# Summing the two halves of the attention output on GpSimd instead of VectorE, in a fused attention and expert kernel

## The chip, the cores and the metric

The kernel runs on one core of one Trainium2 chip. A core has engines with instruction queues of their own: TensorE (PE in the rows, with its weight loads as PEld), VectorE (DVE), ScalarE (ACT), GpSimd (POOL) and SyncE (SP), which here issues nearly all DMAs. Each queue runs strictly in order; engines wait for each other through semaphores. The metric is device time in microseconds (us); lower is better.

## The reference

Attention over 2 batches x 8 heads, 768 positions, head size 64. A position's bucket is the 6-bit sign pattern of its query (or key) times `proj`; a query sees only keys of its own bucket. Two expert layers follow.

```
mask   = q_bucket[:, :, :, None] == k_bucket[:, :, None, :]
scores = scale * q @ k.T, masked with -1e9, softmax over keys
x      = attn @ v                      # to 1536 tokens x 512
h      = (x @ w1) * (x @ w2) @ w3 @ w_out
out    = sum over e of p[:, e] * (relu(h @ e1[e]) @ e2[e])
```

## The kernel before

Every factor is split into a high and a low fp32r part (`hi`, `lo`), and products are made from two or three matmuls of those parts. The attention runs as 48 units (16 heads x 3 blocks of 256 queries). For unit `u`:

- `S` (PE): two tiles of 128 queries x 768 keys of scores into the two `s_ps` buffers. The mask bits sit in extra rows of the operands (`kb`, `ll`), so that a mismatch adds a huge number.
- `mx` (DVE, L443): copies the scores to `e` and takes the row minimum (signs are turned). `ex` (ACT, L446): exponential and row sum. `r1` (POOL, L459), `r2` (DVE, L461) and `en` (POOL L456, or ACT L455 for one tile in four): the normalisation.
- `T` (PE, L477): transposes of `e` into a `t_ps` buffer; `hi` (ACT, L483) and `lo` (DVE, L485) split them into `et`.
- `pv` (PE): twelve matmuls into the one `pv_ps` buffer. The weights are `vv`, which holds the high part of v in 64 columns and the low part in the next 64, so that rows 0 to 63 of `pv_ps` hold one half of the result and rows 64 to 127 the other.
- `po` (ACT, L502) copies the lower half to `pvs`; `xa` (DVE, L504) adds it to the upper half, straight from `pv_ps`, into the token matrix `xt`. The next unit's `pv` waits for `xa`.

Beside that, per head: SP loads q and k (`ld`) and v (`lv`, into `rv`), POOL scales and splits them (L368, L159, L162), and SP copies pieces between partitions (`k1`, `k2`, `k3`, `dq`, L344). Per two heads, `bm` makes the hash products, DVE turns them into bits (`is_pos`, L394), and SP spreads the bits (`mq`, `mk`). For the first head alone, DVE writes them in place. Eight pieces of expert weights are also loaded (`wraw`, L194) and split during the attention (ACT L196 and L208, DVE L198 to L211, POOL L162 and L214). Products of the first expert layer for the first 512 tokens (`fm`, 96 matmuls, tiles `xh` and `slot` into `t_ps` or `s_ps`) are the filler of PE near the end of the attention; `fc` and `fg` (L611) drain them. Then the attention's memory is freed and the expert layers run, first `xh` and `xl` (high and low part of `xt`, L153 and L156), then matmuls into `u_ps` and `o_ps`.

No order is written by hand. Every step is announced with an engine, a planned duration, what it depends on and a due time, which the table `RANK` shifts per group of steps. A list scheduler in `emit_all` then plays this through and emits the instructions in the order that comes out:

```
def op(key, eng, dur, fn, deps, prio, group=None):
    ...
    ops.append((eng, dur, fn, deps, prio + P * RANK.get(group, 0.0), group))
```

Of the kernel before, what the change touches and what calls it, by code (L numbers as in the profile page):

```python
# [13 lines left out]
AF = mybir.ActivationFunctionType  # L14
ALU = mybir.AluOpType
# [12 lines left out]
    "S0": -59.56,  # L28
    "S1": 3.69,
    "T0": -207.42,  # L30
    "T1": -82.6,
    "T2": -31.6,
    "b0": -57.56,
    "b1": -59.96,
    "bits": -7.65,
    "en": 2.75,
    "ex0": -95.56,
    "ex1": -444.49,
    "fd": -89.32,
    "fx": 240.7,  # L40
    "hi0": -7.87,
    "hi1": -248.41,
    "hi2": -157.19,
    "ld": -54.46,
    "lo0": -345.82,
    "lo1": -186.61,
    "lo2": -153.95,
    "lv": -53.81,
    "mx0": -264.79,
    "mx1": -0.59,  # L50
    "p0": -157.78,
    "p1": -422.6,
    "po": -405.44,
    "prep": 73.11,
    "pv": -5.01,
    "r1": -199.11,
    "r2": -270.42,
    "v": 180.48,
# [840 lines left out]
```

## Time and profile before

| | us |
|---|---|
| runs before: median (lowest, highest) of 3 | 1017.81 (1017.12, 1022.36) |
| the profiled execution: its own time | 1020.02 |
| the profiled execution: span from first to last instruction | 1018.2 |
| busy PE, DVE, ACT, POOL | 999.7, 510.1, 362.5, 307.8 |

The busy time is that of whole executions: PE works to the end, while the other engines have most of their work in the attention, which ends near 262 us. Matmuls are pipelined and their ends are modelled, so that a busy PE is not a PE at its peak. In rows on windows, each number of busy us is followed on the chip's page by a number of instructions in brackets; PEclk is the granted TensorE clock as a share of 2.4 GHz.

### The profile page before, as it was taken

What the parts mean: (1) busy time and instruction counts of PE and PEld (TensorE: products, weight loads), DVE (VectorE), ACT (ScalarE), POOL (GpSimd) and SP (SyncE); (2) the same over time, 40 slices, a digit from 0 to 9 for tenths busy, and PEclk for the clock granted to TensorE, in tenths of its full rate; (3) what the DMA queues carried; (4) which work ended last, traced back from release to release, by engine and by line L of the source; (5) the groups of instructions that cost most, each with busy time, mean ns of one, the idle gap of its engine ahead of it and who ended that gap; (6) DMA issues with size and microseconds to landing.
All of it is one profiled execution on the core that took longest, in us unless ns stands there. A gap on an engine that the chain in (4) does not pass through costs nothing.

```text
span 1018.2 us, 13166 instructions
## 1 busy us (share of the span) xinstructions
PE 999.7 (98%) x5035; PEld 844.6 (83%) x5035; DVE 510.1 (50%) x948; ACT 362.5 (36%) x669; POOL 307.8 (30%) x351
## 2 busy tenths in 40 slices
PE   7899999999999999999999999999999999999998
PEld 6888888988788888888888888888888888888886
DVE  6889999998599965954312212121121212212122
ACT  5889999988433322432201101101101101101100
POOL 6777788664000000074300064000650005300000
PEclk9999999999999999999999999999999999999999
DMA  6843544320034321332200032000220002001011
GB/s 162 184 128 77 130 121 112 82 80 21 1 116 127 119 94 49 117 103 63 63 1 1 1 93 73 0 1 1 78 88 1 1 1 73 31 1 42 1 42 42
DMA packets 51135, 64.12 MB, mean 63 GB/s; under 512 B 17688, under 2 KB 34072, under 8 KB 51072
## 3 DMA queue, kind: packets, MB, share of 16 engines
q1 hardware_dynamic: 50928, 63.27, 22.0%
q8 instruction: 40, 0.66, 0.3%
q14 instruction: 23, 0.19, 0.1%
q10 hardware_dynamic: 144, 0.01, 0.0%
HBM read 47.22 MB, written 3.15 MB: 49 GB/s over the span
## 4 chain that ended last, share of the span: by engine, by line
PE 82%; DVE 14%; DMA 1%; ACT 1%; issue 1%; POOL 1%; SPq 0%; DVEq 0%; ACTq 0%; POOLq 0%
PE u_ps L147 43%; PE o_ps L147 30%; DVE et L485 5%; DVE e L443 5%; PE s_ps L147 3%; PE pv_ps L147 2%; PE t_ps L477 2%; PE t_ps L147 2%; DVE xa L504 1%; DVE cbuf L211 1%; DMA wraw<-in_w 1%; ACT e L446 1%; DMA kb<-hh 0%; DVE cbuf L203 0%; DVE cbuf L206 0%
## 5 line engine op out<-in xcount | busy, mean ns | idle before, releaser
L819 DVE SCALAR_TENSOR_TENSOR hl<-u_ps,hl 128x512 fp32r<-128x512 f32 x96 | 66.4, 691 | 420.4 <-ACT hl L817 420.4
L817 ACT ACTIVATE hl<-u_ps 128x512 fp32r<-128x512 f32 x96 | 57.4, 598 | 459.3 <-PE u_ps L147 401.9
L147 PE MATMUL u_ps<-xh,slotl 128*128 128x512 f32 x936 | 220.6, 389 | 0.0
L147 PEld LDWEIGHTS u_ps<-xh,slotl 128*128 128x128 f32 x936 | 175.7, 188 | 36.5
L147 PE MATMUL u_ps<-xh,slot 128*128 128x512 f32 x696 | 165.0, 389 | 1.2 <-DVE xh L156 1.2
L147 PE MATMUL o_ps<-slotl,hl 128*128 128x512 f32 x648 | 154.7, 389 | 0.0
L147 PEld LDWEIGHTS u_ps<-xh,slot 128*128 128x128 f32 x696 | 130.6, 188 | 28.7 <-DVE xh L156 1.6
L147 PEld LDWEIGHTS o_ps<-slotl,hl 128*128 128x128 f32 x648 | 121.6, 188 | 25.2
L147 PE MATMUL o_ps<-slot,hl 128*128 128x512 f32 x504 | 119.9, 389 | 0.0
L147 PEld LDWEIGHTS o_ps<-slot,hl 128*128 128x128 f32 x504 | 94.6, 188 | 19.6
L159 POOL TENSOR_SCALAR slot<-wraw 128x512 fp32r<-128x512 f32 x28 | 17.8, 634 | 286.7 <-PE u_ps L147 269.7
L485 DVE TENSOR_TENSOR et<-t_ps,et 128x512 fp32r<-128x512 f32 x144 | 96.6, 680 | 5.8 <-ACT et L483 5.2
L446 ACT ACTIVATE e<-e,sm 128x768 f32<-128x768 f32 x96 | 89.5, 933 | 12.3 <-DVE e L443 11.0
L147 PE MATMUL pv_ps<-et,vv 128*128 128x256 f32 x576 | 92.8, 297 | 0.8 <-DVE xa L504 0.5
L443 DVE TENSOR_SCALAR_CACHE_REDUCE e<-s_ps 128x768 f32<-128x768 f32 x96 | 90.4, 945 | 4.9 <-PE t_ps L477 3.0
L477 PE MATMUL t_ps<-ident,e 128*128 128x128 f32 x576 | 87.0, 279 | 5.7 <-DVE et L485 4.0
L483 ACT ACTIVATE et<-t_ps 128x512 fp32r<-128x512 f32 x144 | 83.0, 592 | 12.5 <-PE t_ps L477 5.7
L159 POOL TENSOR_SCALAR slotl<-wraw 128x512 fp32r<-128x512 f32 x36 | 22.5, 624 | 208.8 <-PE u_ps L147 172.3
L477 PEld LDWEIGHTS t_ps<-ident,e 128*128 128x128 f32 x576 | 66.3, 142 | 15.9 <-DVE et L485 8.5
L147 PEld LDWEIGHTS pv_ps<-et,vv 128*128 128x128 f32 x576 | 76.0, 192 | 3.0 <-DVE xa L504 2.4
L456 POOL TENSOR_SCALAR e<-e,sm 128x768 f32<-128x768 f32 x72 | 65.5, 916 | 17.4 <-DVE sm L461 15.4
L147 PE MATMUL s_ps<-ka,hh 128*128 128x512 f32 x192 | 53.5, 360 | 3.8 <-issue 2.2
(111 smaller groups left out, 1092.9 us busy)
## 6 DMA issues: line engine op xcount, KB each, us to landing
wraw<-in_e SPq DMA_DIRECT2D x64, 256.0 KB
wraw<-in_w SPq DMA_DIRECT2D x16, 512.0 KB
wraw<-in_w3T SPq DMA_DIRECT2D x16, 512.0 KB
r<-in_qk SPq DMA_DIRECT2D x15, 384.0 KB
wraw<-in_w_out SPq DMA_DIRECT2D x8, 512.0 KB
rv<-in_v SPq DMA_DIRECT2D x16, 192.0 KB
out<-xa SPq DMA_DIRECT2D x12, 256.0 KB
ka<-hh SPq DMA_DIRECT2D x15, 192.0 KB
```

Of the source, the lines that this page charges most:

```text
L147: nc.tensor.matmul(out=o, lhsT=l, rhs=r, start=start, stop=stop)
L159: nc.gpsimd.tensor_scalar(out=o, in0=i, scalar1=1.0, scalar2=1.0, op0=ALU.mult, op1=ALU.mult)
L211: lambda: nc.vector.scalar_tensor_tensor(out=f(t), in0=lw.bitcast(U32), scalar=2.0 ** -52, in1=f(t), op0=ALU.mult, op1=ALU.mult)),
L443: op(("mx", u, t), "DVE", 873, lambda ps=ps, m=m, e=e: nc.vector.tensor_scalar(out=e, in0=ps[:, 0:S], scalar1=THR, scalar2=None, op0=ALU.m ...
L446: op(("ex", u, t), "ACT", 921, lambda e=e, m=m, rs=rs: nc.scalar.activation(out=e, in_=e, func=AF.Exp, scale=-1.0, bias=m, accum_out=rs), ...
L456: return "POOL", 872, lambda: nc.gpsimd.tensor_scalar(out=e, in0=e, scalar1=r[:, t:t + 1], scalar2=1.0, op0=ALU.mult, op1=ALU.mult)
L477: nc.tensor.transpose(out=ps[:, k, t * 128:(t + 1) * 128], in_=e_t[2 * (u % ER) + t][:, kt * 128:(kt + 1) * 128], identity=ident)
L483: op(("hi", n), "ACT", 480, lambda ps=ps, et=et: nc.scalar.activation(out=et[:, 0], in_=ps, func=AF.Copy), [("T", u, j), ("pv", n - NET)], Tj)
L485: op(("lo", n), "DVE", 602, lambda ps=ps, et=et: nc.vector.tensor_tensor(out=et[:, 1], in0=ps, in1=f(et[:, 0]), op=ALU.subtract), [("hi", ...
L504: op(("xa", u), "DVE", 340, lambda: nc.vector.tensor_tensor(out=xt[a, h // 2, t0:t0 + 256], in0=pv_ps[0:D], in1=pvs, op=ALU.add), [("po", ...
L817: op(("gh", n), "ACT", 480, lambda n=n, nu_=nu_: nc.scalar.activation(out=hl_t[n % 2][:, 0], in_=u_ps[nu_ % 4], func=AF.Relu), [ku] + hfre ...
L819: op(("uf", nu_), "DVE", 602, lambda n=n, nu_=nu_: nc.vector.scalar_tensor_tensor(out=hl_t[n % 2][:, 1], in0=u_ps[nu_ % 4], scalar=0.0, in ...
```

## The change

Four things change.

1. `po` now copies all 128 rows of `pv_ps` to a wider `pvs` (three buffers instead of two). A new step `pm` on SP moves the half that lies in the wrong partitions by a DMA from `pvs` to a new buffer `pvd` (two buffers). `xa` adds `pvs` and `pvd` on POOL instead of DVE. The next unit's `pv` waits for `po` alone.
2. v is rearranged on the host, so that `lv` reads 128 rows of 1.5 KB for a head instead of 768 rows of 256 bytes.
3. For the first head, the query bits are written in two pieces (256 columns, then 512), and the second head's low part `l` waits for the first piece. The scores of units 1 and 2 wait for the second.
4. All entries of `RANK` but two, many planned durations and the planned delay after a DMA (2300 ns before, 1900 now) differ, which gives all queues another order.

```diff
-    "xa": -317.88,
+    "pm": -125.95,
+    "xa": -29.47,
...
-    pvs_t = tiles(2, [64, 256], "pvs")
+    pvs_t = tiles(3, [128, 256], "pvs")
+    pvd_t = tiles(2, [128, 256], "pvd")
...
-            ("SP", 1460, [("cd", n - NRAW), ("c2", n - NRAW)], "cl",
+            ("SP", 2700, [("cd", n - NRAW), ("c2", n - NRAW)], "cl",
...
-        "SP": {"PE": 2300, "ACT": 2300, "DVE": 2300, "POOL": 2300, "SP": 2300, "NONE": 0},
+        "SP": {"PE": 1900, "ACT": 1900, "DVE": 1900, "POOL": 1900, "SP": 1900, "NONE": 0},
...
-                op(("l", hh), "DVE", 870, lambda: scaled_lo(nc.vector), [("h", hh)], T, g)
+                op(("l", hh), "DVE", 1000, lambda: scaled_lo(nc.vector), [("h", hh), ("mq", 0)], T, g)
...
-        op(("lv", hh), "SP", 600, lambda: nc.sync.dma_start(out=rv, in_=v[b, h].rearrange("(k p) d -> p k d", p=128)),
+        op(("lv", hh), "SP", 1000, lambda: nc.sync.dma_start(out=rv, in_=v[b, h].rearrange("p (k d) -> p k d", k=NK)),
...
-        op(("mq", 0), "DVE", 865, lambda: is_pos(lo[64:64 + PC], ps, q), [("mk", 0)], T, "b0")
-        keys[("sf", n)] = keys[("mq", 0)]
+        for i, (key, c) in enumerate(((("mq", 0), slice(0, 256)), (("sf", n), slice(256, S)))):
+            op(key, "DVE", (330, 600)[i], lambda c=c: is_pos(lo[64:64 + PC, c], ps, q, c), [("mk", 0)], T + i, "b0")
...
-            op(("pv", n), "PE", 472, lambda j=j: pv(j), [("lo", n), ("vl", hh), ("xa", u - 1), ("pv", n - 1)], Tp)
+            op(("pv", n), "PE", 472, lambda j=j: pv(j), [("lo", n), ("vl", hh), ("po", u - 1), ("pv", n - 1)], Tp)
...
-        op(("po", u), "ACT", 264, lambda: nc.scalar.activation(out=pvs, in_=pv_ps[D:2 * D], func=AF.Copy),
-           [("pv", NJ * u + NJ - 1), ("xa", u - 2)], Tp)
-        op(("xa", u), "DVE", 340, lambda: nc.vector.tensor_tensor(
-            out=xt[a, h // 2, t0:t0 + 256], in0=pv_ps[0:D], in1=pvs, op=ALU.add), [("po", u)], Tp)
+        w, t0 = h % 2, b * S + qp * 256
+        a, o = slice(w * D, (w + 1) * D), slice((1 - w) * D, (2 - w) * D)
+        op(("po", u), "ACT", 283, lambda: nc.scalar.activation(out=pvs, in_=pv_ps, func=AF.Copy),
+           [("pv", NJ * u + NJ - 1), ("xa", u - 3)], Tp)
+        op(("pm", u), "SP", 500, lambda: nc.sync.dma_start(out=pvd[a], in_=pvs[o]), [("po", u), ("xa", u - 2)], Tp)
+        op(("xa", u), "POOL", 520, lambda: nc.gpsimd.tensor_tensor(
+            out=xt[a, h // 2, t0:t0 + 256], in0=pvs[a], in1=pvd[a], op=ALU.add), [("pm", u)], Tp)
...
-        "v": v,
+        "v": v.reshape(v.shape[0], v.shape[1], -1, 128, D).swapaxes(2, 3).reshape(v.shape[0], v.shape[1], 128, -1),
```

What the new order looks like is shown at three places. The first is DVE's queue at the start: `ll_85` and `ll_86` are the low parts of heads 0 and 1, `kb_93` takes the key bits of head 0, and `e_99` the first scores. Before:

```order
L347 SCALAR_TENSOR_TENSOR ll_85<-r_114,svec,hh_81 128x768
L347 SCALAR_TENSOR_TENSOR ll_86<-r_115,svec,hh_82 128x768
L394 TENSOR_SCALAR kb_93<-s_ps_129,thr,amp 12x768
L394 TENSOR_SCALAR ll_85<-s_ps_129,thr,amp 12x768
L443 TENSOR_SCALAR e_99,sm_122<-s_ps_130 128x768
```

And in the changed kernel:

```order
L349 SCALAR_TENSOR_TENSOR ll_85<-r_117,svec,hh_81 128x768
L396 TENSOR_SCALAR kb_93<-s_ps_132,thr,amp 12x768
L396 TENSOR_SCALAR ll_85<-s_ps_132,thr,amp 12x256
L396 TENSOR_SCALAR ll_85<-s_ps_132,thr,amp 12x512
L349 SCALAR_TENSOR_TENSOR ll_86<-r_118,svec,hh_82 128x768
L446 TENSOR_SCALAR e_99,sm_125<-s_ps_133 128x768
```

The low part of head 1 has moved from ahead of the bits to behind them, and the query bits have become two instructions.

The second place is POOL's queue in the middle of the attention, around units 20 and 21, while the q and k of head 10 and the v of head 7 are split. `sm` is `r1`, `e` is `en`, `ll` and `hh` are the parts of q and k, `vv` those of v. Before:

```order
L459 TENSOR_SCALAR sm_124<-sm_124 128x2
L162 TENSOR_TENSOR ll_87<-r_114,hh_83 128x768
L456 TENSOR_SCALAR e_103<-e_103,sm_124 128x768
L159 TENSOR_SCALAR vv_98<-rv_116 128x6x64
L162 TENSOR_TENSOR vv_98<-rv_116,vv_98 128x6x64
L459 TENSOR_SCALAR sm_125<-sm_125 128x2
L456 TENSOR_SCALAR e_99<-e_99,sm_125 128x768
L456 TENSOR_SCALAR e_100<-e_100,sm_125 128x768
```

In the changed kernel:

```order
L510 TENSOR_TENSOR xa<-pvs_110,pvd_112 64x256
L164 TENSOR_TENSOR vv_98<-rv_119,vv_98 128x6x64
L462 TENSOR_SCALAR sm_127<-sm_127 128x2
L161 TENSOR_SCALAR hh_83<-r_117 128x768
L459 TENSOR_SCALAR e_103<-e_103,sm_127 128x768
L510 TENSOR_TENSOR xa<-pvs_111,pvd_113 64x256
L164 TENSOR_TENSOR ll_87<-r_117,hh_83 128x768
L462 TENSOR_SCALAR sm_128<-sm_128 128x2
L370 TENSOR_SCALAR r_118<-r_118,svec 128x768
L164 TENSOR_TENSOR xh_66<-xa,xh_66 128x512
```

One `xa` for each unit now stands among the same steps, and the `r1` and `en` of later units stand behind it.

The third place is PE's queue where the attention ends: the last `pv` (`vv_98`), the rest of the filler (`xh_66`), and the first product of the expert layers (`u_ps`). Before:

```order
L147 MATMUL pv_ps<-et_108,vv_98 128x256 x4
L147 MATMUL t_ps_134<-xh_66,slot_64 128x512 x12
L147 MATMUL s_ps_129<-xh_66,slot_64 128x512 x5
L147 MATMUL t_ps_134<-xh_66,slot_65 128x512 x12
L147 MATMUL s_ps_129<-xh_66,slot_64 128x512 x4
L147 MATMUL t_ps_134<-xh_66,slot_65 128x512 x12
L147 MATMUL u_ps_3041<-xh_3022,slot_62 128x512 x12
```

In the changed kernel:

```order
L149 MATMUL pv_ps<-et_108,vv_98 128x256 x4
L149 MATMUL t_ps_137<-xh_66,slot_63 128x512 x12
L149 MATMUL s_ps_132<-xh_66,slot_64 128x512 x5
L149 MATMUL t_ps_137<-xh_66,slot_64 128x512 x12
L149 MATMUL s_ps_132<-xh_66,slot_64 128x512 x5
L149 MATMUL t_ps_137<-xh_66,slot_65 128x512 x24
L149 MATMUL u_ps_3093<-xh_3074,slot_62 128x512 x12
```

58 filler matmuls instead of 45 are left behind the last `pv`, and the last two groups of twelve, which use one buffer, now follow each other directly.

## Rows read from the trace of the kernel before

**Rows 1.** The page: busy us (share of the span) xinstructions, by engine.

```profile
PE 999.7 (98%) x5035; PEld 844.6 (83%) x5035; DVE 510.1 (50%) x948; ACT 362.5 (36%) x669; POOL 307.8 (30%) x351
```

**Rows 2.** Windows: us, busy PE, PEld, DVE, ACT, POOL, PEclk, DMA, GB/s.

```profile
94.00:136.00 42.00, 40.64 (x294) 36.53 (x293) 41.71 (x89) 37.58 (x76) 34.32 (x41) 1.00 0.49 115
136.00:178.00 42.00, 41.18 (x305) 37.99 (x304) 41.61 (x91) 40.41 (x81) 34.30 (x42) 1.00 0.48 119
178.00:220.00 42.00, 41.65 (x299) 37.98 (x298) 41.66 (x90) 39.20 (x79) 27.52 (x34) 1.00 0.33 80
220.00:262.40 42.40, 41.90 (x288) 36.67 (x287) 36.22 (x72) 32.61 (x63) 18.18 (x24) 1.00 0.10 31
```

**Rows 3.** The chain that ended last, 100 to 112 us: start us, us, what.

```profile
104.01 1.20 DVE et L485 x2
105.21 0.33 DVE xa L504
...
108.83 0.42 DVE xa L504
```

**Rows 4.** Groups by line and shape, 94 to 220 us.

```profile
L485 DVE TENSOR_TENSOR et<-t_ps,et 128x512 fp32r<-128x512 f32 x77 | 51.7, 678 | 0.2
...
L504 DVE TENSOR_TENSOR xa<-pv_ps,pvs 64x256 f32<-64x256 f32 x26 | 10.7, 412 | 0.4
...
L162 POOL TENSOR_TENSOR ll<-r,hh 128x768 fp32r<-128x768 f32 x7 | 12.9, 1843 | 0.6
...
L162 POOL TENSOR_TENSOR xh<-xa,xh 128x512 fp32r<-128x512 f32 x2 | 2.6, 1298 | 0.0
...
L502 ACT ACTIVATE pvs<-pv_ps 64x256 f32<-64x256 f32 x26 | 9.9, 381 | 0.8
```

**Rows 5.** Timeline of the start: start us, us, engine, line, op.

```profile
5.92 1.02 DVE L347 SCALAR_TENSOR_TENSOR ll<-r,svec,hh 128x768 fp32r<-128x768 f32 x1 [1.33 <-ACT hh L352]
...
6.31 0.94 ACT L364 ACTIVATE hh<-r,svec 128x768 fp32r<-128x768 f32 x1 [0.42 <-DMA r<-in_qk]
...
7.28 2.17 DVE L347 SCALAR_TENSOR_TENSOR ll<-r,svec,hh 128x768 fp32r<-128x768 f32 x1 [0.34 <-ACT hh L364]
...
7.57 0.28 PE L147 MATMUL s_ps<-ll,pbh 128*128 128x256 f32 x1
...
8.66 0.94 ACT L358 ACTIVATE hh<-r,svec 64x768 fp32r<-64x768 f32 x1 [1.42 <-POOL ka L162]
...
11.71 0.62 PE L147 MATMUL s_ps<-kb,ll 76*128 76x512 f32 x2 [1.43 <-DVE ll L394]
...
12.37 0.96 DVE L443 TENSOR_SCALAR_CACHE_REDUCE e<-s_ps 128x768 f32<-128x768 f32 x1 [0.71 <-PE s_ps L147]
```

**Rows 6.** Timeline, 34 to 41 us.

```profile
34.80 0.52 SPq L344 DMA_DIRECT2D hh<-hh  x1
...
38.43 0.58 PE L147 MATMUL s_ps<-ka,hh 128*128 128x512 f32 x2 [2.16 <-issue]
```

**Rows 7.** Windows of the two stalls; columns as in rows 2.

```profile
36.00:42.00 6.00, 3.79 (x20) 3.29 (x19) 3.19 (x7) 2.24 (x5) 2.90 (x3) 0.81 1.11 217
66.00:69.00 3.00, 1.51 (x11) 1.01 (x9) 0.80 (x4) 1.13 (x2) 2.92 (x3) 1.00 0.29 63
```

**Rows 8.** Timeline, 60 to 76 us.

```profile
61.60 0.37 SPq L194 DMA_DIRECT2D wraw<-in_w  x1
...
67.87 0.67 ACT L196 ACTIVATE cbuf<-wraw 128x512 f32<-128x512 f32 x1 [2.66 <-DMA wraw<-in_w]
```

**Rows 9.** Timeline of the end of attention.

```profile
266.38 2.88 PE L147 MATMUL t_ps<-xh,slot 128*128 128x512 f32 x12
...
269.10 1.07 PE L147 MATMUL s_ps<-xh,slot 128*128 128x512 f32 x4
...
273.23 0.69 DVE L611 TENSOR_TENSOR g<-g,t_ps 128x512 f32<-128x512 f32 x1 [3.18 <-PE t_ps L147]
...
274.57 5.72 PE L147 MATMUL u_ps<-xh,slot 128*128 128x512 f32 x24 [1.22 <-DVE xh L156]
```

More of the change, by code (lines that the diff above doesn't have):

```diff
@@ L27 @@
     "CP": 16.1,
[L28 to L58, printed above, removed]
-    "xa": -317.88,
+    "S0": -71.69,
+    "S1": 65.66,
+    "T0": -210.57,
+    "T1": -24.46,
+    "T2": -166.93,
+    "b0": -120.38,
+    "b1": -78.37,
+    "bits": -313.13,
+    "en": -33.99,
+    "ex0": 115.81,
+    "ex1": -102.2,
+    "fd": -80.92,
+    "fx": 220.7,
+    "hi0": -232.84,
+    "hi1": -141.31,
+    "hi2": -183.33,
+    "ld": -79.23,
+    "lo0": -215.67,
+    "lo1": -88.66,
+    "lo2": -54.12,
+    "lv": -78.2,
+    "mx0": -123.92,
+    "mx1": -40.8,
+    "p0": -23.71,
+    "p1": -252.6,
+    "pm": -125.95,
+    "po": -198.02,
+    "prep": -24.15,
+    "pv": 67.79,
+    "r1": -141.28,
+    "r2": -505.14,
+    "v": -326.75,
+    "xa": -29.47,
 }
@@ L209, in conv64 @@
             (side, sdur, [("ch", n)], "cp", lambda: minus(lo_(), f(c), hi_())),
-            ("DVE", 602, [("c3", n)], "cd",
+            ("DVE", 700, [("c3", n)], "cd",
              lambda: nc.vector.scalar_tensor_tensor(out=f(t), in0=lw.bitcast(U32), scalar=2.0 ** -52, in1=f(t),
@@ L360, in head @@
         else:
-            op(("ld", hh), "SP", 1130, lambda: load(slice(0, 2 * D)), [("l", hh - RR)] if hh >= RR else [],
+            op(("ld", hh), "SP", 2000, lambda: load(slice(0, 2 * D)), [(x, hh - RR) for x in (("l", "k1", "k2", "k3", "dq") if hh == RR else ("l",))],
                -1e9 + 1e7 * hh if first else T - 8000)
             if first:
-                op(("h", hh), "ACT", 733, lambda: nc.scalar.activation(out=hi, in_=r, func=AF.Copy, scale=svec),
+                op(("h", hh), "ACT", 830, lambda: nc.scalar.activation(out=hi, in_=r, func=AF.Copy, scale=svec),
                    [("ld", hh), ("sv", 0)], T, g)
-                op(("l", hh), "DVE", 870, lambda: scaled_lo(nc.vector), [("h", hh)], T, g)
+                op(("l", hh), "DVE", 1000, lambda: scaled_lo(nc.vector), [("h", hh), ("mq", 0)], T, g)
             else:
@@ L441, in unit @@
             Tt = T + t * P / 2
-            op(("S", u, t), "PE", 690, score, [(k, hh) for k in ("mq", "mk", "k1", "k2", "k3", "dq")] + free_, Tt)
+            op(("S", u, t), "PE", 690, score, [(k, hh) for k in ("mq", "mk", "k1", "k2", "k3", "dq")] +
+               ([("sf", 0)] if 0 < u < NQ else []) + free_, Tt)
             op(("mx", u, t), "DVE", 873, lambda ps=ps, m=m, e=e: nc.vector.tensor_scalar(
@@ L457, in norm @@
                 out=e, in0=e, scalar1=r[:, t:t + 1], scalar2=1.0, op0=ALU.mult, op1=ALU.mult)
-        op(("r1", u), "POOL", 300, lambda: nc.gpsimd.tensor_scalar(
+        op(("r1", u), "POOL", 295, lambda: nc.gpsimd.tensor_scalar(
             out=sm[:, 0:2], in0=sm[:, 6:8], scalar1=1e-9, scalar2=None, op0=ALU.add), ex, T + 2 * P)
```

28 lines of the change are left out of this document (14 added, 14 removed).

## The prediction

> **What bounds the kernel now.** I read the page's busy times first, then windows over the attention, then the chain, groups and timeline of the places that the change touches. PE is busy for 999.7 of 1018.2 us [rows 1]. From 274.57 us on [rows 9] PE runs the expert layers, which the change doesn't touch. So the question is how much earlier that point comes.
>
> In the windows from 94 to 220 us [rows 2] DVE is busy for 41.6 to 41.7 of 42 us: 124.98 of 126 us in the three. ACT has 117.19 and POOL 96.14. PE shows 123.47, but its matmuls overlap, so I don't take that for a full engine. In the chain [rows 3] one DVE instruction follows another without a gap, `xa` among them at 0.33 to 0.42 us. DVE is the bound here, and `xa` is part of it: 26 instructions, 10.7 us [rows 4].
>
> Earlier the bound is another. Between 36 and 42 us DVE works 3.19 of 6 us, and PE's clock is at 0.81 on average [rows 7]; the score matmuls start at 38.43 us after 2.16 us of idleness [rows 6]. The page names no releaser; they need the copy that SP issued at 34.80, so I read it as that copy's landing, 3.6 us after issue, with the DMA engines full (share 1.11 [rows 7]). Between 66 and 69 us DVE works 0.80 of 3 us: ACT waits 2.66 us, in order, for a weight load issued at 61.60 and used at 67.87, 6.3 us later, and in that time DVE, which follows ACT, stands too [rows 7, 8]. The two stalls cost DVE 2.81 + 2.20 = 5.0 us. From 220 to 262.4 us PE is busy for 41.90 of 42.40 us and DVE for 36.22 [rows 2]; there PE fills its gaps with filler.
>
> **The change, part by part.**
>
> *`xa` leaves DVE.* Over the 126 us from 94 to 220, DVE loses 26 x 0.33 = 8.6 us (the shorter step in the chain) to 10.7 us (the group), so it needs 114.3 to 116.4. But ACT still has its 117.2 us: `po` reads 128 partitions instead of 64 with the same 256 columns, and I price the wider one at nothing, since ACT took 0.94 us for 768 columns on 128 partitions and on 64 [rows 5]; at worst it costs twice 0.381 us [rows 4], 9.9 us more. And POOL takes `xa` over. No row shows it. Two subtractions of two SBUF operands on POOL take 1843 ns for 768 columns and 1298 for 512 [rows 4]: 2.13 ns a column, so 256 columns are 1.298 - 0.545 = 0.75 us. The bounds are 0.65 us (half of 1298) and 1.30 (no shorter at all). I take 0.75, the line through both rows. That is 26 x 0.75 = 19.5 us, and POOL stands at 115.6. So DVE, ACT and POOL would need 114 to 117 of today's 126 us. At most 126 - 117.2 = 8.8 us can be saved, and three engines that feed one another in order will not all run without a gap. I choose half, 4.4 us, or 0.17 us a unit. The stretches from 44 to 61 and 76 to 94 us hold 35 / 4.85 = 7 more units (126 us for 26 units is 4.85): another 1.2 us. From 220 on, DVE isn't full, and I count nothing. Sum **-5.6 us**, bounds 0 and -(8.8 + 7 x 0.34) = -11.2.
>
> POOL's row for 512 columns, 1298 ns, stands against 678 for a DVE instruction of that size [rows 4], 1.9 times as long. The Trainium skill, GPSIMD Engine Reference, Engine selection, says to use VectorE for an elementwise sum, since GpSimd is about twice as slow with two inputs; the trace agrees. By that rule alone `xa` would cost POOL twice 0.412 us, 21.4 us in the 126, and the move, which gives back twice what it frees, should not pay; by the rows it costs 19.5 us on an engine that has 30 of 126 us free. The rule is a rival below.
>
> `pv` no longer waits for `xa` but for `po`; what PE waited there is inside the same 4.4 us. The new DMA `pm` is off the path as long as `xa` isn't needed: its readers are `fh`, much later, and `po` three units on, 3 x 4.85 = 14.5 us after, against a landing of 3.6 to 6.3 us [rows 6, 8]. Behind a waiting `pm` in SP's queue stand the next head's loads and copies; behind a waiting `xa` in POOL's stand `r1` and `en` of later units, for which PE's transposes wait. 48 more issues at 0.52 us [rows 6] are 25 us of SP's 260.
>
> *v in 1.5 KB rows, and SP's new order.* A load of v goes from 768 descriptors to 128. The first weight load goes from the 20th to the 42nd place in SP's queue, out of the crowd around 36 us. The planned time from a weight load's issue to its use goes from 1.46 + 2.30 to 2.70 + 1.90 us, 0.84 more, where the trace shows 6.3: by that alone 1.8 of ACT's 2.66 us would stay. Against it, two weight loads now stand almost side by side in SP's queue, and ACT takes them directly one after the other. The stalls may go or move. I take half of their 5.0 us: **-2.5 us**, bounds 0 and -5.0.
>
> *The start.* DVE's low part of head 1 takes 2.17 us from 7.28, where head 0's took 1.02 [rows 5]. It now comes after the bits. They can start when the hash products end, 7.57 + 0.28 = 7.85 us, and take some 2.3 to 2.5 us (11.71 - 9.45 was 2.26). Then the low part takes 1.02 to 2.17, and the first `mx` starts at 11.2 to 12.5 instead of 12.37 [rows 5]. I take **-0.5 us**, bounds -1.2 and +0.2.
>
> *The end.* 58 filler matmuls instead of 45 follow the last `pv`. Twelve take 269.10 - 266.38 = 2.72 us [rows 9], so 13 take 2.95. They are missing before it, where PE was full, so most of it is only moved: **+1.0 us**, bounds 0 and 2.95. The last two groups now share a buffer with nothing between them, so that PE waits for one DVE drain of 0.69 us [rows 9] and its handover: **+0.8 us**. The last `xa` now takes a DMA and POOL, some 4.5 us at 3.6 + 0.75. It is hidden by the 7.7 us of filler (34 matmuls) ahead of ACT's first conversion. If that cover went, the difference would be paid in full.
>
> Sum: -5.6 - 2.5 - 0.5 + 1.0 + 0.8 = -6.8 us. The profiled execution took 1020.0 us (1018.2 of span and 1.8 around it), so 1013.2 for its like. It lies 2.2 us above the median of the runs shown; against that median the forecast is 1017.8 - 6.8 = **1011.0 us**.
>
> **Rivals.**
>
> *The other engines are as full as DVE.* POOL has 68.6 of 84 us from 94 to 178 [rows 2]; 17.3 units of 0.75 us make it 81.6, 97%. With `en` in the chain of each unit, POOL would then be the bound, and DVE's time comes back as waits for POOL. This is what the skill's rule amounts to. Steady part -1.0 instead of -5.6, half as much from the stalls: -1.0 - 1.2 - 0.5 + 1.8 = -0.9, so 1016.9 us. For it: the 97%, and PE's 98%. Against: the weight pieces, which make POOL full there, can stand elsewhere, and from 178 on POOL has 27.5 of 42.
>
> *POOL stops for `pm`.* `xa` waits at the head of POOL's queue for a DMA that the plan takes to land 1.9 us after issue, and rows show 3.6 and more. POOL has (84 - 68.6) / 17.3 = 0.89 us a unit to spare: once `xa` with its wait costs more than that, the kernel gets slower. At 0.75 + 0.35 = 1.10 us POOL needs 87.7 for 84 us, +3.7, and about +2 over 42 to 94 us; with -0.5, -1.2 and +1.8 that is +5.8, so 1023.6 us. For it: in-order POOL, one SP queue. Against: `xa` stands about a unit, 5 us, behind its `pv` in POOL's queue.
>
> *More goes than I count.* Both stalls vanish (-5.0), the steady part is at its bound (-11.2), the start too (-1.2), the end as above: -15.6, so 1002.2 us. For it: DVE ran at 99% for 126 us, so full queues are possible here. Against: three floors within 3 us.
>
> **How the numbers follow.** Chances: forecast 0.57, full engines 0.21, POOL stops 0.13, more 0.09. The forecast's own range is 1006 to 1015 us. The range for all reaches to the full-engine case and part of the way to the large gain: 1002.5 to 1018.5 leaves out POOL's stops and part of the last case, under 2 in 10. I take 0.5%, 5.1 us, as what a measurement of this kernel can tell from no change. Faster than 1012.7: 0.50 of the forecast and the large gain, 0.59. Slower than 1022.9: 0.12. The rest, 0.29, is the same.
>
> **What would show it.** Right: in windows of 42 us between 94 and 220, more than 8.7 units each; DVE near 91 to 95%, POOL 90% or more; `xa` on POOL near 0.75 us with little idleness before it; no wait of 2 us for a weight load on ACT; 58 fillers after the last `pv`; the first `u_ps` some 7 us before 274.57. Wrong: DVE idle for POOL's `r1` or `en`, `xa` waiting for a DMA, `po` at over 0.5 us, or ACT's wait for a weight load in a new place. A table with an order that makes PE wait for buffers would also break the forecast, and the trace before can't show that.

## The result, and the profile after

The changed kernel takes 1027.5 us (median of 5 runs, 1026.6 to 1028.0) against 1017.4 of the kernel before on the same chip (5 runs, 1016.9 to 1022.4): ratio 1.0085 (1.0061 to 1.0108). It is slower, where 1011.0 was forecast. Its profiled execution took 1026.66 us, with a span of 1024.9 (before 1018.2). The two profiled executions differ by 6.6 us and the medians by 10.1, since the profile of the kernel before took 2.6 us more than its median and that of the changed kernel 0.9 us less. The traces below account for the 6.7 us of span, and not for the whole 10.1.

The page of the changed kernel, to set against [rows 1]:

```profile
PE 997.7 (97%) x5035; PEld 843.6 (82%) x5035; DVE 509.2 (50%) x901; ACT 356.4 (35%) x669; POOL 345.5 (34%) x399
```

Its windows over the attention, against [rows 2]:

```profile
94.00:136.00 42.00, 38.22 (x271) 33.78 (x270) 41.17 (x78) 35.00 (x74) 39.35 (x46) 1.00 0.54 139
136.00:178.00 42.00, 37.35 (x273) 33.95 (x272) 41.06 (x76) 35.02 (x74) 38.45 (x44) 1.00 0.45 122
178.00:220.00 42.00, 37.40 (x260) 34.25 (x259) 40.38 (x74) 34.10 (x69) 36.03 (x44) 0.96 0.33 83
220.00:262.40 42.40, 42.40 (x306) 39.09 (x305) 32.44 (x65) 34.80 (x70) 24.50 (x34) 1.00 0.08 22
```

`xa` has left DVE, and yet DVE is busy for 122.6 of the 126 us up to 220, nearly as before. ACT fell to 104 us, which shows that fewer units pass, and POOL rose to 114. The groups from 94 to 220 us by line and shape show `xa` on POOL and what fills DVE, the `cbuf` lines above all, the steps that split expert weights. Changed kernel:

```profile
L488 DVE TENSOR_TENSOR et<-t_ps,et 128x512 fp32r<-128x512 f32 x70 | 45.6, 677 | 0.0
...
L510 POOL TENSOR_TENSOR xa<-pvs,pvd 64x256 f32<-64x256 f32 x24 | 18.8, 788 | 1.2 <-DVE sm L464 0.3
...
L213 DVE SCALAR_TENSOR_TENSOR cbuf<-wraw,cbuf 128x512 f32<-128x512 uint32 x6 | 9.7, 1623 | 0.0
L202 DVE TENSOR_SCALAR cbuf<-cbuf 128x512 int32<-128x512 int32 x6 | 6.1, 1024 | 0.0
L205 DVE SCALAR_TENSOR_TENSOR cbuf<-wraw,cbuf 128x512 int32<-128x512 int32 x5 | 6.0, 1194 | 0.0
L208 DVE TENSOR_SCALAR cbuf<-cbuf 128x512 int32<-128x512 int32 x6 | 5.6, 932 | 0.0
L200 DVE TENSOR_SCALAR cbuf<-cbuf 128x512 f32<-128x512 f32 x6 | 5.4, 896 | 0.0
```

The same weight steps in the kernel before (L200 there is L202 here, and so on):

```profile
L211 DVE SCALAR_TENSOR_TENSOR cbuf<-wraw,cbuf 128x512 f32<-128x512 uint32 x6 | 7.1, 1181 | 0.0
...
L206 DVE TENSOR_SCALAR cbuf<-cbuf 128x512 int32<-128x512 int32 x6 | 3.9, 653 | 0.0
L203 DVE SCALAR_TENSOR_TENSOR cbuf<-wraw,cbuf 128x512 int32<-128x512 int32 x5 | 3.7, 735 | 0.0
L200 DVE TENSOR_SCALAR cbuf<-cbuf 128x512 int32<-128x512 int32 x5 | 2.1, 420 | 0.0
L198 DVE TENSOR_SCALAR cbuf<-cbuf 128x512 f32<-128x512 f32 x4 | 1.7, 427 | 0.0
```

26 of these steps took 18.5 us before; 29 now take 32.8. The 14.3 us more exceed the 10.7 of `xa` [rows 4]. The steps got longer (0.71 us on average, now 1.13), while `lo`, which reads PSUM, stayed (678 and 677 ns). The timeline of the changed kernel from 155 us shows one such step:

```profile
155.50 1.28 POOL L164 TENSOR_TENSOR slot<-cbuf,slot 128x512 fp32r<-128x512 f32 x1
...
155.84 3.02 DVE L202 TENSOR_SCALAR cbuf<-cbuf 128x512 int32<-128x512 int32 x1
...
156.74 1.83 POOL L164 TENSOR_TENSOR ll<-r,hh 128x768 fp32r<-128x768 f32 x1
...
158.55 0.67 POOL L161 TENSOR_SCALAR vv<-rv 128x384 fp32r<-128x384 f32 x1
...
158.89 0.87 DVE L205 SCALAR_TENSOR_TENSOR cbuf<-wraw,cbuf 128x512 int32<-128x512 int32 x1
...
159.69 0.94 DVE L446 TENSOR_SCALAR_CACHE_REDUCE e<-s_ps 128x768 f32<-128x768 f32 x1
...
160.69 0.61 PE L149 MATMUL s_ps<-ka,hh 128*128 128x512 f32 x2 [2.35 <-DVE e L446]
```

Behind the attention, where POOL stands idle, the same shift takes 0.41 us:

```profile
283.73 0.41 DVE L202 TENSOR_SCALAR cbuf<-cbuf 128x512 int32<-128x512 int32 x1
```

At 155.84 it starts 0.34 us after POOL's `slot` step and ends 3.02 us later, when POOL is through with `slot` and `ll` and in the middle of `vv`. `mx` stands behind it in DVE's queue, and PE waits 2.35 us for `mx`. The Trainium skill, SBUF — State Buffer, Who interferes with whom, says that a VectorE step with two SBUF inputs contends with a GpSimd step that reads SBUF, and that of a VectorE step in a two-port mode and a GpSimd step the one issued first holds the shared ports for its whole length while the other is blocked. The steps on PSUM (unchanged) and those on `cbuf` (longer) agree; but here the wait outlasted two whole GpSimd steps and part of a third.

The start, against [rows 5], went as told: the low part of head 1 takes 1.02 us, and the first `mx` starts at 11.05 us (12.37 before).

```profile
10.11 1.02 DVE L349 SCALAR_TENSOR_TENSOR ll<-r,svec,hh 128x768 fp32r<-128x768 f32 x1
...
11.05 0.95 DVE L446 TENSOR_SCALAR_CACHE_REDUCE e<-s_ps 128x768 f32<-128x768 f32 x1
```

The end of the attention, against [rows 9], and the one new kind of wait in the expert layers:

```profile
274.20 3.06 PE L149 MATMUL t_ps<-xh,slot 128*128 128x512 f32 x12 [0.85 <-DVE g L617]
...
278.71 1.64 PE L149 MATMUL u_ps<-xh,slot 128*128 128x512 f32 x6 [1.23 <-DVE xh L158]
```

```profile
425.68 0.60 ACT L155 ACTIVATE slotl<-u_ps 128x512 fp32r<-128x512 f32 x1 [0.81 <-PE u_ps L149]
...
426.33 1.92 PE L149 MATMUL o_ps<-hl,slotl 128*128 128x512 f32 x6 [0.69 <-ACT slotl L155]
```

PE waits 0.85 us between the last two filler groups, the first long group on `u_ps` starts at 278.71 instead of 274.57, and at 426.33 (and once more at 452) PE waits for ACT.

To place the time, I mark the start of `po` (the copy of a finished `pv_ps`) of some units in each trace:

| profile | po of unit 8 | units 8 to 38 | last matmul of pv | filler after it | steps on cbuf, units 8 to 38 |
|---|---|---|---|---|---|
| before | 74.6 | 143.8 | 262.4 | 45 | 25, 18.0 us |
| after | 66.7 | 156.3 | 262.6 | 58 | 36, 36.8 us |

So the changed kernel is 7.9 us ahead at unit 8, loses 12.5 us up to unit 38, and gains 4.4 back to unit 47. Two runs below tell how well this repeats. e15 keeps the order of before up to unit 8 and far beyond, and its `po` of unit 8 starts at 72.9 us; e12 keeps the changed order up to the last `pv` and has 66.8, with 156.1 us for units 8 to 38. The lead is thus 6.1 to 7.9 us, while the loss repeats within a few tenths.

PE's clock has a part in the lead. In the kernel before, PE stood for 2.16 us ahead of 38.43 us and for 2.29 us ahead of 69.80, and both times its granted clock was then at 1.2 GHz for a stretch (PEclk about 0.5; columns as in [rows 2]):

```profile
39.70:43.10 3.40, 3.40 (x17) 3.31 (x16) 2.22 (x6) 1.63 (x3) 0.90 (x2) 0.50 1.04 276
```

```profile
70.40:73.80 3.40, 3.40 (x17) 3.21 (x16) 2.64 (x7) 3.27 (x6) 0.64 (x2) 0.51 0.94 259
```

In the changed kernel it was at 2.4 GHz from the first matmuls until 194 us (see e9).

At the last `pv` the two profiles are even. The rest comes behind it: 13 more fillers at 0.227 us (2.95 us), the wait between fillers (0.85, and some 0.1 of slower start), and 2.5 us in the expert layers. 0.2 + 2.95 + 0.95 + 2.5 = 6.6 of the 6.7 us of span.

### The profile page after: what moved, and what is told of

It is laid out like the page before. It is cut to its first block, busy times and chain, and to the rows that moved or that the text cites. A ratio compares the mean times of both kernels' runs of the same rounds, so it can differ in the third digit from the quotient of the medians.

```text
span 1024.9 us, 13349 instructions
## 1 busy us (share of the span) xinstructions
PE 997.7 (97%) x5035; PEld 843.6 (82%) x5035; DVE 509.2 (50%) x901; ACT 356.4 (35%) x669; POOL 345.5 (34%) x399
## 4 chain that ended last, share of the span: by engine, by line
PE 85%; DVE 6%; POOL 5%; issue 2%; ACT 1%; DMA 1%; POOLq 0%; DVEq 0%; ACTq 0%
PE u_ps L149 42%; PE o_ps L149 30%; PE s_ps L149 4%; PE t_ps L480 3%; PE pv_ps L149 3%; PE t_ps L149 2%; DVE et L488 2%; DVE e L446 2%; POOL e L459 1%; POOL xa L510 1%; POOL ll L164 1%; PE t_ps L538 1%; DVE bt L396 0%; DVE cbuf L202 0%; POOL vv L164 0%
## 5 line engine op out<-in xcount | busy, mean ns | idle before, releaser
L149 PEld LDWEIGHTS u_ps<-xh,slot 128*128 128x128 f32 x696 | 130.5, 188 | 28.7 <-DVE xh L158 1.6
L488 DVE TENSOR_TENSOR et<-t_ps,et 128x512 fp32r<-128x512 f32 x144 | 94.0, 680 | 5.8 <-ACT et L486 5.4
L449 ACT ACTIVATE e<-e,sm 128x768 f32<-128x768 f32 x96 | 89.7, 936 | 12.9 <-DVE e L446 12.5
L480 PE MATMUL t_ps<-ident,e 128*128 128x128 f32 x576 | 82.8, 276 | 9.0 <-DVE et L488 6.5
L149 PE MATMUL pv_ps<-et,vv 128*128 128x256 f32 x576 | 90.7, 295 | 0.0
L459 POOL TENSOR_SCALAR e<-e,sm 128x768 f32<-128x768 f32 x72 | 67.6, 945 | 8.7 <-DVE sm L464 6.6
```

The costliest lines, as they stand in the source:

```text
L149: nc.tensor.matmul(out=o, lhsT=l, rhs=r, start=start, stop=stop)
L449: op(("ex", u, t), "ACT", 921, lambda e=e, m=m, rs=rs: nc.scalar.activation(out=e, in_=e, func=AF.Exp, scale=-1.0, bias=m, accum_out=rs), ...
L459: return "POOL", 872, lambda: nc.gpsimd.tensor_scalar(out=e, in0=e, scalar1=r[:, t:t + 1], scalar2=1.0, op0=ALU.mult, op1=ALU.mult)
L480: nc.tensor.transpose(out=ps[:, k, t * 128:(t + 1) * 128], in_=e_t[2 * (u % ER) + t][:, kt * 128:(kt + 1) * 128], identity=ident)
L488: op(("lo", n), "DVE", 602, lambda ps=ps, et=et: nc.vector.tensor_tensor(out=et[:, 1], in0=ps, in1=f(et[:, 0]), op=ALU.subtract), [("hi", ...
```

## The experiments

All numbers on units are read from the traces as above; ratios are to runs of the kernel before on the same chip.

**Undo the move: e1.** `po`, `xa` and `pv`'s wait as before, in the changed kernel:

```diff
-        op(("xa", u), "POOL", 520, lambda: nc.gpsimd.tensor_tensor(
-            out=xt[a, h // 2, t0:t0 + 256], in0=pvs[a], in1=pvd[a], op=ALU.add), [("pm", u)], Tp)
+        op(("xa", u), "DVE", 340, lambda: nc.vector.tensor_tensor(
+            out=xt[a, h // 2, t0:t0 + 256], in0=pv_ps[0:D], in1=pvs, op=ALU.add), [("po", u)], Tp)
```

> The changed kernel with the sum of the halves back on VectorE as in the kernel before (the halves summed from PSUM, no transfer, pv waits for xa again, the two rank numbers of po and xa as before); the v rows, the early bits, the other rank numbers and the planned durations stay. Theory 1 (contention: VectorE's weight-splitting steps from SBUF to SBUF wait out GpSimd's two-input steps, of which xa is a new one per unit): the early gain of 5 to 9 us stays, the steps on cbuf take about 27 us between 30 and 245 us again in place of 40, and the time is 1010 to 1016 us. Theory 2 (the new table of ranks and planned durations is itself the worse order from unit 13 on): the loss of some 14 us between units 13 and 37 stays, 1023 to 1029 us. Theory 3 (wait for the transfer): like theory 1 in time, but the steps on cbuf are no shorter.

1026.0 us, ratio 1.0083 (1.0068 to 1.0098): theory 2's number. Units 8 to 38 take 155.6 us, and 156.3 with the sum on GpSimd, although the steps on `cbuf` fell to 26.8 us there (32 of them). So the new table without any move is 11.8 us slower in this stretch than the kernel before. The last `pv` comes 3.4 us before that of the kernel before, but 64 fillers follow it. The new table does not suit the sum on DVE, then; whether the planner would have found better numbers for it is not told.

**The move alone, planned anew: e2.** The lines of the change on `pvs`, `pvd`, `po`, `pm` and `xa` in the kernel before.

> The kernel before with the sum moved to GpSimd by way of the transfer and nothing else (ranks for pm and xa as in the changed kernel). Theory 1 (contention): VectorE loses 412 ns of xa in each unit and gets longer steps on cbuf, 35 to 42 us between 30 and 245 us in place of 27; the time is 1017 to 1030 us, no faster than before. Theory 2 (order): the move by itself is worth what was forecast for it, 1007 to 1014 us. Theory 3 (transfer): slower, with pv or xa seen waiting for pm.

1061.7 us, 1.0433 (1.0415 to 1.0451). With these ranks the planner's order is so poor (GpSimd waits 15.3 us for transfers, DVE 21.1 for `hi`) that the run tells little of the move. In the runs that follow, every engine keeps its order but for what is named.

**The wait for the transfer: e3.** `in1=pvd[a]` becomes `in1=pvs[a]`.

> The changed kernel with xa reading its own half of pvs twice in place of the transferred half; the transfer is still made and the order of every engine is the same, only the wait for it is gone (the output then lacks one half of each sum). Theories 1 and 2: within 3 us of the changed kernel, 1024 to 1029 us. Theory 3 (GpSimd stops for the transfer): 1014 to 1020 us.

1023.4 us, 1.0057 (1.0040 to 1.0074), the last `pv` 3.8 us earlier than in the changed kernel, units 8 to 38 in 153.2. That lies between the theories: the wait costs 3.8 us at most, not all. It may be less, since `xa` also became shorter in e3 (0.65 us on average from 94 to 220 us, 0.79 in the changed kernel). From 27 to 290 us of the changed kernel, GpSimd stood for transfers as this row says, and only 2.5 us of it, one wait at 221.4 us, lies ahead of unit 38:

```profile
POOL xa L510 <- DMA pvd<-pvs: 8.9, 5, 2.9
```

How the 3.8 us divide between the wait and the shorter `xa` is not told.

**One input at a time: e4.**

```diff
-        in0=pvs[a], in1=pvd[a], op=ALU.add
+        for o_ in (xt[a, h // 2, t0:t0 + 256], pvd[a]):
+            nc.gpsimd.tensor_scalar(out=o_, in0=pvd[a], scalar1=1.0, scalar2=1.0, op0=ALU.mult, op1=ALU.mult)
```

> The changed kernel with xa made of two one-input steps on the transferred half, in place of one two-input step: GpSimd is as busy as before (about 0.7 us for each unit), waits for the same transfer, in the same order, but reads one operand at a time (the output then lacks the other half of each sum). Theory 1 (two-input steps of GpSimd hold up VectorE's SBUF steps): the steps on cbuf fall from 40 us to 32 to 36 us between 30 and 245 us (ll, xh and the weight steps on GpSimd still have two inputs), and the time is 1018 to 1024 us. Theory 2 and theory 3: no change, 1025 to 1029 us.

1034.4 us, 1.0162 (1.0147 to 1.0177): slower than all theories said, and the steps on `cbuf` stayed at 41.8 us (30 to 245 us). That `xa` has two inputs is not what makes them long. The pair takes about 0.84 us of POOL instead of 0.79 for each unit and moves the last `pv` back by 7.9 us; why so much is open.

**Weight steps with one SBUF operand: e5 (changed kernel) and e6 (before).** For the first eight tiles, the five DVE steps read the strided `wraw` alone:

```diff
-             lambda: nc.vector.tensor_scalar(out=t, in0=c, scalar1=3, ...
+             lambda: nc.vector.tensor_scalar(out=t, in0=hw, scalar1=3, ...
```

> The changed kernel with the five weight-splitting steps of VectorE that run beside the attention (the first 8 tiles) each reading one strided SBUF operand, wraw, in place of cbuf or of two operands; same order on every engine, same GpSimd steps (the split weights are then not those of the reference). Theory 1 (contention): such steps take some 0.68 us each whatever GpSimd does, 27 us in all between 30 and 245 us in place of 41.5, the last pv comes 6 to 13 us earlier, and the time is 1014 to 1021 us. Theory 4 (GpSimd's own added 0.79 us for each unit sets the pace, as the 0.1 us for each unit more of the one-input run, 7 us in all, suggests): VectorE's time does not matter, 1024 to 1029 us.

> The kernel before with the same edit as e5. Its steps on cbuf take 28.7 us between 30 and 245 us and should take about 27. Theory 1: 1013 to 1018 us, so that the changed kernel loses most of its distance in e5, within 5 us of this run. Theory 4: 1015 to 1019 us, and e5 stays 7 to 11 us behind it.

The premise failed: undisturbed, such a step took 0.41 us, as fast as on contiguous data, and beside POOL it stood as long as ever (groups of e5, then of e6, 94 to 220 us):

```profile
L195 DVE TENSOR_SCALAR cbuf<-wraw 128x512 int32<-128x512 int32 x19 | 16.8, 886 | 0.0
```

```profile
L193 DVE TENSOR_SCALAR cbuf<-wraw 128x512 int32<-128x512 int32 x17 | 8.0, 479 | 0.0
```

The same step took 479 ns in the order of before and 886 in the new one. e5: 1022.9 us, 1.0040 (1.0023 to 1.0058), last `pv` 3.8 us earlier; e6: 0.9996 (0.9980 to 1.0013). What the kernels take without that contention stays unmeasured.

**The rows of v alone: e7.** The two lines on `v` in the kernel before.

> The kernel before with v laid out in 1.5 KB rows and nothing else; the order of every engine is that of before. If the stalls at 36 and 66 us come from the transfers of v in small packets, the unit that ends at 74.6 us ends 3 to 7 us earlier. Theory 5 (a lead gained early stays): 1010 to 1015 us. Theory 6 (a lead is used up in the steady part, where the order is bound by its weight tiles or by VectorE): 1016 to 1019 us.

0.9998 (0.9987 to 1.0008), no difference. In the trace unit 8 ends 1.7 us earlier, but so it does in e15, where nothing is changed up to there, so that the rows of v are not shown to bring anything. The early lead comes from elsewhere, then.

**A shorter `xa`: e8.** 8 columns instead of 256, added in place where the transfer lands.

> The changed kernel with xa cut to 8 of its 256 columns on GpSimd (the transfer lands in the result's own rows, and the other columns lack one half); same order, same transfer, same wait, but some 0.2 us of GpSimd for each unit in place of 0.79. Theory 4 (GpSimd's added time sets the pace): the last pv comes 10 to 20 us earlier, 1007 to 1017 us. Theory 1: GpSimd's shorter step leaves less to wait for, but ll, xh and the weight steps stay: cbuf 32 to 40 us, 1018 to 1025 us. Theory 2 (the order itself): 1022 to 1027 us.

1017.4 us, 0.9986 (0.9977 to 0.9996); the last `pv` 8.2 us earlier than in the changed kernel, units 8 to 38 in 150.3 us, 33.6 us of them on `cbuf`. That is less than the 10 to 20 us of theory 4, but GpSimd's time for `xa` costs 6.0 of the 12.5 us. The other 6.5 remain with `xa` nearly gone from both engines. GpSimd's wait for the transfer, which e8 still makes, is 1.6 us of the stretch; the rest I put down to the order, which has 36 weight steps there. That is what is left over, and no run measures the order of the changed kernel by itself.

**Two of forty weight steps left out: e9.** `n != 4 and` ahead of the shift, `n != 5 and` ahead of the product, in `conv64`.

> The changed kernel without two of its forty weight-splitting steps of VectorE beside the attention, the two that stand still longest behind GpSimd's steps: the shift of weight tile 4 (3.02 us at 155.84, 0.42 alone) and the product of tile 5 (3.34 us at 188.63, 0.68 alone); everything else in the same order (two eighths of the early split weights are then a little wrong). Theory 1 (such holds are what the changed kernel loses): the steps of 4 to 6 us in the distance to before between units 24 and 26 and between 30 and 32 go, the last pv comes 5 to 9 us earlier, 1017 to 1022 us. Theory 4 and theory 2: only their own 1.1 us, 1024 to 1027 us, or the hold passes to the next step on cbuf.

1023.6 us, 1.0042 (1.0027 to 1.0057), last `pv` 3.6 us earlier, for steps of 1.1 us. In units 8 to 38 the steps on `cbuf` fell by 3.4 us: the hold partly passed to the next one. So holds cost time, but these two explain 3.6 us, less than the 5 to 9 that theory 1 wanted.

The second hold cost more than its own time. In the changed kernel PE stood for 1.85 us behind it:

```profile
188.63 3.34 DVE L213 SCALAR_TENSOR_TENSOR cbuf<-wraw,cbuf 128x512 f32<-128x512 uint32 x1
...
192.91 0.62 PE L149 MATMUL s_ps<-ka,hh 128*128 128x512 f32 x2 [1.85 <-DVE e L446]
```

Then its granted clock was at 1.2 GHz, while in e9 it stayed at 2.4 GHz throughout. The same window in the changed kernel, then in e9:

```profile
194.10:197.50 3.40, 3.40 (x18) 3.39 (x17) 3.37 (x10) 2.79 (x6) 2.22 (x3) 0.50 0.58 181
```

```profile
194.10:197.50 3.40, 3.40 (x28) 2.95 (x26) 3.40 (x6) 3.40 (x7) 3.40 (x5) 1.00 0.32 94
```

18 matmuls instead of 28 in 3.4 us are worth some 1.2 us, by an estimate that takes the matmuls as alike.

**More DVE: e10.** In the first `mx` of a unit, of the changed kernel:

```diff
+                if t == 0:
+                    nc.vector.tensor_scalar(out=e[0:64, 0:256], in0=ps[0:64, 0:256], scalar1=THR, scalar2=None, op0=ALU.min)
```

> The changed kernel with one more VectorE step of the size of the old xa for each unit (64x256 from PSUM, about 0.41 us, 20 us in all, just ahead of the first mx; it writes what mx writes over). Same order, correct result. It prices VectorE's time in the changed kernel's order. Theory 7 (VectorE is the bound there, and what its freed 20 us brought was lost elsewhere): the last pv comes 10 to 20 us later, 1036 to 1047 us. Theory 4 (GpSimd sets the pace now): 0 to 5 us later, 1026 to 1031 us.

1041.8 us, 1.0222 (1.0205 to 1.0239), last `pv` 15.1 us later for 19.5 us of DVE (48 steps of 0.405 us): theory 7. Time on DVE is paid for in the changed kernel too, at 0.77 us for each us.

**The relief alone: e11.** In the kernel before, ACT copies straight into the result, and DVE adds 8 of 256 columns.

> The kernel before with xa on VectorE cut to 8 of 256 columns (ScalarE's copy goes straight into the result's rows; the other columns lack one half): 0.41 us for each unit become about 0.1, some 15 us of VectorE in all, with GpSimd, the order and the DMA queues untouched. It measures the steady term of the forecast alone. By the forecast's share (5.6 us for 20 us) it brings 4 to 5 us, up to 9 by its bound: 1009 to 1014 us. Theory 2 (the order's other engines are as full): 1015.5 to 1018.5 us.

1017.2 us, 0.9979 (0.9967 to 0.9990); this is theory 2's number. In its trace the last `pv` comes 5.5 us earlier, 3.1 of them before unit 8, where e15 differs by 1.7 with nothing changed. In units 8 to 38 `xa` falls from 12.4 to 4.6 us, and the stretch gets 1.8 us shorter; the steps on `cbuf` take 20.2 us there (26 of them) instead of 18.0 (25). So 7.8 us less on DVE bring 0.23 us for each, where e10 pays 0.77 for each us more. That fits other engines that are nearly as full, which these two runs alone do not show.

**Old durations behind the attention: e12.** `2700 if beside else 1460` and so on in `conv64`.

> The changed kernel, with the planner's old durations for the weight tiles that are split after the attention (from the ninth on), so that the order differs there alone. If the two waits of the down-projections at 425 and 451 us come from the new durations, they go, and with them 2.5 us: 1023 to 1025.5 us. If they come from anything else: 1026 to 1028 us.

1025.0 us, 1.0056 (1.0041 to 1.0071). Both waits in the expert layers are gone: from the last `pv` to the last matmul 755.7 us instead of 758.2.

**Weight steps moved by hand: e13 to e16.** After the planning, tiles 5, 6 and 7 are taken out of the order and put behind the `mx` of units 38 to 46, each step up to a unit after the one it needs (the loads two units ahead).

> The changed kernel with the splitting of weight tiles 5, 6 and 7 (15 steps of VectorE, with their loads and their steps of ScalarE and GpSimd) moved behind the mx of units 38 to 46; all else in the order of the changed kernel, correct result. Theory 8 (the place of these steps in a stretch where VectorE is the bound is what the change loses): 15 steps of about 1 us each as they stand there, at the 0.79 us that a us of VectorE cost in e10, bring the last pv 8 to 12 us earlier: 1014 to 1019 us. Theory 4 (GpSimd's xa and the transfer set the pace by themselves): 0 to 4 us, 1022 to 1026 us.

> e13 together with the old durations for the weight tiles after the attention (e12, which took 2 us). Theory 8: 1011 to 1017 us, below the kernel before for the first time with the sum on GpSimd. Theory 4: 1020 to 1024 us.

> The kernel before with the same three weight tiles moved in the same way (the seventh lies there already); its VectorE has only 25 of these steps between units 8 and 38, at 0.72 us each, and TensorE has gaps of only 2.9 us there. Theory 8: 10 steps less bring 1 to 3 us, 1014.5 to 1017.5 us. If the place of the steps is worth as much here as in the changed kernel: 1008 to 1012 us.

> e1 (the changed kernel with the sum on VectorE, 1026.0 us) with the three tiles moved and the old durations after the attention. Theory 8: what holds the changed order back is the 32 steps between units 8 and 38, not where the sum is made: 1014 to 1019 us, near e14. Theory 4: the sum on VectorE is then better than on GpSimd, 1008 to 1014 us, 5 us or more below e14.

All are slower than the kernel before and than theory 8 said: e13 1.0137 (1.0114 to 1.0160), e14 1.0109 (1.0085 to 1.0133), e15 1.0072 (1.0050 to 1.0094), e16 1.0136 (1.0114 to 1.0157). At unit 34 e13 is 4.6 us ahead of the changed kernel, and it loses 9 from there to the end, where ACT now waits three times for DVE's `cbuf` (8.0 us). Theory 8 as I put it has fallen: the idle time of DVE near the end is not free for these steps, or my places were bad; the two are not told apart.

**The move in the old order: e17 and e18.** The kernel before in its own order; `pm` is issued right behind `po`, and `xa` stands on GpSimd two `mx` later. e18 reads `pvs` twice, so that it does not wait for the transfer.

```diff
+            if key[0] == "po":
+                pm_of[key[1]]()
+                queue.append((mxs if mxs < 2 * NU else -9, xa_of[key[1]], ...))
```

> The kernel before in its own order on every engine, with the sum moved: ScalarE copies all 128 rows, the transfer is issued right behind the copy, xa leaves VectorE's row and stands on GpSimd two mx later; correct result. The forecast's steady term with none of the rest: e11 (the same relief of VectorE without a cost on GpSimd) gained 5 us in its profile and 1.8 in the medians, so 1012 to 1017 us if GpSimd takes the sum at no cost. Theory 4 (GpSimd's added time costs what e8 showed, 8 us for 27.6 us, so some 11 us for 37, and the wait for the transfer 3.6 as in e3): the two come to some 14 us less the 2 to 5 of relief, 1025 to 1031 us.

> e17 with xa reading its own half twice, the transfer made but not waited for (the output lacks one half of each sum). Theory 4 with the price of e3: 3 to 5 us below e17. If the transfer's wait is the whole cost of the move: back at 1012 to 1017 us. If it never ends last: within 1.5 us of e17.

e17: 1056.6 us, 1.0384 (1.0366 to 1.0401), far above every expectation. e18: 1025.7 us, 1.0079 (1.0064 to 1.0094), 31 us below e17, which none of its expectations said. DVE's waits for `r1` (`sm`) from 27 to 290 us: kernel before, changed kernel, e18, e17 (us, times, longest), and then the waits of `xa` in e17:

```profile
DVE sm L461 <- POOL sm L459: 1.1, 1, 1.1
```

```profile
DVE sm L464 <- POOL sm L462: 9.6, 13, 1.3
```

```profile
DVE sm L475 <- POOL sm L473: 14.6, 18, 2.1
```

```profile
DVE sm L475 <- POOL sm L473: 38.7, 24, 3.8
```

```profile
POOL xa L522 <- DMA pvd<-pvs: 21.4, 17, 3.8
```

In e17 `xa` stops GpSimd for 21.4 us. `r1` stands behind it, and DVE waits 38.7 us for `r1`. Without that wait (e18) DVE still waits 14.6 us, its `cbuf` steps take 35.8 us instead of 28.7 (30 to 245 us), and units 8 to 38 take 149.1. In this order the move is a loss even without the wait for its transfer, and with an `xa` of 0.64 us instead of 0.79.

DVE's own time in units 8 to 38 tells how the loss comes about: kernel before, changed kernel, e18 (us, busy DVE, PEclk, DMA, GB/s), and then the waits of DVE for `r1` in the same stretch, in the changed kernel and in e18 (in the kernel before there is none):

```profile
74.60:218.40 143.80, 142.35 (x303) 1.00 0.42 101
```

```profile
66.70:223.00 156.30, 151.37 (x285) 0.99 0.44 118
```

```profile
74.80:223.90 149.10, 138.61 (x274) 1.00 0.46 113
```

```profile
DVE sm L464 <- POOL sm L462: 2.1, 4, 0.7
```

```profile
DVE sm L475 <- POOL sm L473: 7.4, 10, 1.0
```

In all, `xa` took 12.4 us off DVE. In the changed kernel the steps on `cbuf` put 18.8 back: by an estimate from the table above, 7.9 for eleven more steps at the old 0.72 us, and 10.9 because each of the 36 takes 1.02. The wait for `r1` is small there, 2.1 us. In e18 the steps on `cbuf` put 7.5 us back (26 instead of 25, in 25.5 us), and the wait for `r1` is 7.4.

## Why the prediction was wrong

**The steady term failed, and in its sign.** I had -5.6 us, from 0.17 us a unit, so -5.1 for 30 units; units 8 to 38 took +12.5. Its steps:

- *DVE is the bound, and `xa` is part of it*: right, but the gain was priced too high. e10 prices DVE at 15.1 us for 19.5 more; e11 shows that the relief by itself is a gain, but of 1.8 us for 7.8 less, or 0.23 for each, where I had 4.4 for 10.7, or 0.41.
- *`xa` takes 0.75 us on POOL*: right, 0.788 measured in the 126 us.
- *It costs nothing there, since POOL has 30 of 126 us free*: the step that failed. I added up the engine's time and did not ask what stands behind `xa`. In the old order the move cost 5.3 us in units 8 to 38 with no wait for the transfer (e18), where relief alone brought 1.8 (e11); in the new order `xa`'s time costs 6.0 (e8). Two ways are seen: `r1` comes later, and DVE's SBUF steps stand behind a busier POOL. In DVE's own time the second is the larger one in the changed kernel (10.9 us of longer steps, by the estimate under e18, against 2.1 us of waits for `r1`), and the two are alike in e18 (7.5 and 7.4). How much of the longer steps is due to `xa` itself is not shown: in e8, with `xa` nearly gone from POOL, the 36 steps still take 33.6 of the 36.8 us.
- *`pm` is off the path*: wrong by at most 3.8 us in the changed kernel (e3), by some 31 in the old order (e17 against e18); in both pairs the shorter `xa` is counted in.
- *The order stays what it was, but for the places named*: wrong. The new table puts 36 weight steps into units 8 to 38 instead of 25. With the table and no move the stretch is 11.8 us slower than before (e1), and with `xa` cut short 6.5 us of loss remain there (e8). That the eleven more steps are the cause was argued, not shown: e13, with 28 of them, takes 152.9 us instead of 156.3 there (with no stretch at 1.2 GHz), but loses more behind it. What in the order costs this time stays open.

**Stalls and start were right in kind and too small.** I had -2.5 and -0.5. The first `mx` came 1.3 us earlier, ACT waited for no weight load up to 100 us, and unit 8 came 6.1 to 7.9 us earlier, as much as both bounds together (6.2) or more. PE's clock, at 1.2 GHz behind both stalls of the kernel before, had no term in the sum. Part of the lead was a loan: 4 weight steps lie ahead of unit 8 instead of 8, and the others came later. The v rows, which I put into this term, moved no time that can be told (e7).

**The end was mis-sized.** The drain gap, 0.8, measured 0.85. The fillers took 2.95 us behind the last `pv`, their bound. Ahead of it the changed kernel gained 4.4 us from unit 38 to 47, where it has 39 fillers instead of 47 and no weight steps instead of 7; how much of that the missing fillers brought, and so whether +1.0 was right, is not told. And the expert layers, "which the change doesn't touch", lost 2.5 us to the planner's new durations (e12); the sum had no term for it.

**The rivals.** "The other engines are as full" named one of the two ways, GpSimd before `r1`, which is seen in the old order (e18) more than in the changed kernel; DVE's weight steps held up behind GpSimd stood in no rival. By the rule beside it (the Trainium skill, GPSIMD Engine Reference, Engine selection: elementwise sums belong on VectorE) the move should not pay, which e18 bears out at 1.0079. But I priced it at a lost gain, 1016.9, not at a loss. "POOL stops for `pm`", 1023.6, lay nearest in time, by luck: its reason, the wait for the transfer, is worth 3.8 us at most (e3).

## What to carry to other kernels

Price a step on an engine with idle time by what stands behind it in that queue, not by the idle share: here 0.64 us of GpSimd for each unit, put into a queue that makes `r1` and beside VectorE's steps on SBUF, cost more than 0.41 us of the full VectorE gave back (e18). When a table that sets an order changes, count the steps of each kind per stretch in both orders, the parts that the edit does not name included. A lead in an early stage counts only if the work that used to fill its stalls has not been pushed into the full stage behind.

## What the hardware showed unexpectedly

- A VectorE step from SBUF to SBUF that takes 0.42 us alone stood for 3.02 us, through two GpSimd steps that followed each other without a gap and into a third; another, 0.68 us alone, for 3.34. The step did not end between them.
- Reading one SBUF operand with a stride of two elements did not avoid this: 0.41 us undisturbed, 0.886 on average in e5. Steps that read PSUM (`lo`, 0.68 us) did not change.
- A GpSimd step of two SBUF inputs of 64x256 took 0.788 us on average (0.75 from the line through 512 and 768 columns), and two one-input steps of that size 0.84.
